# Row scans of the later sets in two halves, and weight blocks converted at one pace

## The chip, the cores and the metric

The kernel runs on one core of a Trainium2 chip. The metric is the device time of one execution in microseconds (us). The core has five engines that run unsynchronised, each with its own queue of instructions in program order: TensorE (PE; its weight loads are listed as PEld), VectorE (DVE), ScalarE (ACT), GpSimd (POOL) and SyncE (SP), which here only issues transfers (DMA).

## What is computed

Two stages, all in float32. The first is a recurrence over 768 steps for 4 x 8 heads of width 40; the second a two-layer MLP ("MoE" in the names) on 3072 rows of 320:

```python
for t in range(S):
    y[:, :, t] = np.einsum('bhd,bhde->bhe', rt, state)
    Sa = np.einsum('bhde,bhe->bhd', state, at)
    state = state * wt[:, :, None, :] - np.einsum('bhd,bhe->bhde', Sa, bt) + np.einsum('bhd,bhe->bhde', vt, kt)
x = y.transpose(0, 2, 1, 3).reshape(B * S, H * D)
h = x @ w_in                                     # 320 -> 2048
g = np.where(h >= 1, h, np.where(h <= -1, 0.0, (h + 1) ** 2 / 4))
out = g @ w_out                                  # 2048 -> 320
```

## The kernel before

The recurrence is done in 24 chunks of 32 steps. Six sets of four chunks are prepared one after the other, each in three stages. *Rows* (`prelude`, L241): for each of four parts of eight steps, the running products P of w and their reciprocals come from two scans on VectorE, forward and reversed, over a tile of 40 groups of 10 columns (`scan`, L227, its instruction is L235); zeros at both ends of a group restart the product, so the 40 groups do not depend on each other. GpSimd multiplies a, k and b by the results (L273, L281, L289) and stores the part to DRAM (`scr`, L290). *ab*: rows are loaded back from `scr` (L304), transposed (L325), multiplied pairwise on TensorE (L336) and copied to `pairs` (L343). *inv*: a triangular inversion of `pairs`, for sets 1 and on as 62 products and differences on GpSimd (L363, L369); `adopt` (L376) puts its result in place for the next four chunks.

The chain of the recurrence (`chain`, L504, one generator for each chunk and half of the heads) and the MoE (`moe`, L628) run beside this. The MoE takes 64 steps at a time; a step k of it makes `ph` on TensorE (L637), the gate on ACT, DVE, ACT and POOL (L647, L648, L650, L653 for `gh`, L654 for `gl`), and then 12 second products (L668) with the two weight blocks `w2_2k` and `w2_2k+1`, of step k - 1, whose last four need `gl`.

Weights arrive as 64-bit floats and are converted in 28 blocks (`weights`, L742; 12 of `w_in`, then 16 of `w_out`, named `w2_0` to `w2_15`). A block is two ACT instructions (L751, L755), one on DVE (L759), a cast on ACT (L771) and the low part on POOL (L772; some early ones on DVE); it ends two blocks later in the program than it begins, and its end issues the raw load of the block five ahead (L739, on SP).

Everything is emitted in one order by hand. The main loop calls `fill` (L917) four times a chunk; a fill advances the clock `now` by 2.5 and has six turns. In each turn it emits MoE matmuls, advances the weight generator when the sum of `PACE` says so (each block is three such steps), and calls `background` (L411). That takes the stage that is furthest behind its due share in its window (`WINDOWS`) and runs its generator to the next `yield`, whose value counts as work done; `size` is a stage's total. If the MoE's first group needs a block that is not yet converted, it advances the weight generator itself (`needs`).

Of the kernel before, what the change touches and what calls it, by code (L numbers as in the profile page):

```python
# [20 lines left out]
NB, NHD, D, L = 4, 8, 40, 32  # L21
# [7 lines left out]
    rows=[(0, 0), (24, 43), (46, 64), (70, 90), (106, 130)],  # L29
    ab=[(0, 0), (44, 55), (68, 84), (95, 119), (135, 159)],  # L30
    inv=[(2, 28), (55.5, 79), (85, 118), (121, 158), (161, 198)],
)

AHEAD = 5
PACE = (0.8, 1.0)

SHARE = (1.4, 0.6) * 2
SLOTS = len(SHARE)
# [1 line left out]
ROWS_W = (2, 2, 4, 2, 6, 6, 8)  # L40
AB_W = (6, 26, 6, 3, 8, 30)
INV_W = 12
INV_STEP = [0.45 + (j + 1) * (31 - j) / 256 for j in range(31)]
# [12 lines left out]
def rwkv_moe_kernel(ctx: ExitStack, tc: tile.TileContext, r, k, v, w, a, b, w_in, w_out, ident_d, mask_d, out):  # L56
# [28 lines left out]
    wz = const.tile([128, D, 10], F32, name="wz")  # L85
    dz = const.tile([128, D, 10], F32, name="dz")
# [49 lines left out]
    def copy_rv(s, part, c, n=1):  # L136

        x, o = ((r, O_R), (v, O_V))[part]
        nc.sync.dma_start(
            scr[s][0 : NH * 128].rearrange("(h x) e -> h x e", x=128)[:, L * c : L * (c + n), o : o + D],  # L140
            x.rearrange("b h t e -> (b h) t e")[:, 128 * s + L * c : 128 * s + L * (c + n), :],
        )
# [84 lines left out]
    def scan(out, d0, d1, step=1):  # L227


        def line(x):  # L230
            x = x.rearrange("p e t -> p (e t)")
            (pp, pn), (st, n) = x.ap
            return x if step == 1 else bass.AP(x.tensor, x.offset + (n - 1) * st, [[pp, pn], [-st, n]])

        nc.vector.tensor_tensor_scan(  # L235
            out=line(out), data0=line(d0), data1=line(d1), initial=0.0, op0=ALU.mult, op1=ALU.add
        )
# [3 lines left out]
    def prelude(s):  # L241

        R = arena.rearrange("p (t x) -> p t x", x=160)
        kt, P, at, bt = (R[:, :, 40 * i : 40 * i + 40] for i in range(4))
        rows_ = lambda x: x.rearrange("p e t -> p t e")

        def load(n, s, part):
            if n == "w":
                t = work.tile([128, 10 * D], F32, tag="ld_w", name="ld_w")
            else:  # L250
                t = work.tile([128, 8 * D], F32, tag="ld_x", name=f"ld_{n}", bufs=2)
            x = t[:, 0 : 8 * D].rearrange("p (t e) -> p t e", e=D)
            nc.sync.dma_start(x, srcs[n][:, 4 * s : 4 * s + 4, 8 * part : 8 * part + 8, :])
            return (t, x) if n == "w" else x

        wl, al, kl = ahead.pop(s) if s in ahead else [load(n, s, 0) for n in "wak"]
        yield 10
        for part in range(4):
            ts_ = slice(8 * part, 8 * part + 8)
            then = (s, part + 1) if part < 3 else (s + 1, 0)  # L260
            more = then[0] < NS
            nc.scalar.copy(rows_(wz)[:, 1:9], wl[1])
            yield ROWS_W[0]
            Pc = wl[0].rearrange("p (e t) -> p e t", t=10)
            if part == 0:
                nc.vector.memset(dz[:, :, 0], -1.0)
            scan(Pc, wz, dz)
            yield ROWS_W[1]
            if part < 3:
                nc.vector.tensor_copy(dz[:, :, 0], Pc[:, :, 8])  # L270
            nc.vector.reciprocal(dz[:, :, 9], Pc[:, :, 8])
            nc.scalar.copy(P, rows_(Pc)[:, 1:9])
            nc.gpsimd.tensor_mul(at, al, rows_(Pc)[:, 0:8])  # L273
            yield 1
            scan(wz, wz, dz, -1)
            rec = rows_(wz)[:, 2:10]
            copy_rv(s, 0, part)
            yield ROWS_W[2]
            bl = load("b", s, part)
            yield ROWS_W[3]  # L280
            nc.gpsimd.tensor_mul(kt, kl, rec)  # L281
            if more:
                wl = load("w", *then)
            yield ROWS_W[4]
            if more:
                al = load("a", *then)
            copy_rv(s, 1, part)
            yield ROWS_W[5]
            nc.gpsimd.tensor_mul(bt, bl, rec)  # L289
            nc.gpsimd.dma_start(scr[s][0 : NH * 128, 80:240].rearrange("(p t) x -> p t x", t=L)[:, ts_, :], R)  # L290
            nc.gpsimd.memset(wz[:, :, 0::9], 0.0)
            yield ROWS_W[6]
            if more:
                kl = load("k", *then)
        if more:
            ahead[s + 1] = wl, al, kl
# [82 lines left out]
    def staged(key, needs, work_of):  # L379
        for s in range(2 if key != "inv" else 0, NS):  # L380
            if needs:
                drain(needs, s)
            total = 0
            for d in work_of(s):
                total += d
                yield d
            if s:
                size[key] = total
            done[key] = s
            yield 0  # L390

    turned_in, turned_out = set(), set()
    done, size, spent = dict(rows=1, ab=1), dict(rows=10 + 4 * (1 + sum(ROWS_W)), ab=2 * AB_W[5] + 4 * AB_W[0] + 8 * (2 + sum(AB_W[1:4])), inv=INV_W + 2 * sum(INV_STEP)), {}
    back = {k: staged(*a) for k, a in dict(
        rows=("rows", None, prelude), ab=("ab", "rows", ab_set), inv=("inv", "ab", invert)).items()}

    def drain(key, s):
# [13 lines left out]
    def background(n):  # L411

        due = []
        for key in ("inv", "ab", "rows"):
            for s in range(1, NS):
                a, b = window(key, s)
                if a < n <= b:
                    drain(key, s - 1)
                    at = spent.setdefault((key, s), [0])
                    due.append((key, s, at, size[key] * (gone(n) - gone(a)) / (gone(b) - gone(a))))  # L420
        while True:
            due = [(k, s, at, to) for k, s, at, to in due if done[k] < s and at[0] < to]
            if not due:
                return
            key, _, at, _ = max(due, key=lambda x: x[3] - x[2][0])
            at[0] += next(back[key])
# [368 lines left out]
    def pull(gen, n=1):  # L795
        for _ in range(n):
            if next(gen, "end") == "end":
                return False
        return True
# [94 lines left out]
    now = [0]  # L894
    due = [0]
# [5 lines left out]
    def feed(cols):  # L901

        if not Xs:
            return
        owed[0] += cols * (not idle[0])
        while owed[0] > 0:
            d = next(mgen)
            owed[0] = 0 if d is None else owed[0] - d
            idle[0] = d is None

    def catch_up():

        for f in deferred:
            f()
        deferred.clear()

    def fill():  # L917

        catch_up()
        for k in range(6):  # L920
            feed(1280)
            if first:
                first.pop(0)()
            due[0] += PACE[now[0] >= 20]
            while due[0] > 0:
                pull(wgen)
                due[0] -= 1
            background(now[0] + 10 / SLOTS * (k + 1) / 6)
        now[0] += 10 / SLOTS

    for c in range(NC + 1):
# [9 lines left out]
        if c < NC:  # L941
            if c and c % 4 == 0:
                adopt(c // 4)
            for j in (0, 1) if c else (2, 0, 1):
                turn(c, 1, j)
        fill()
        stage(c - 1, 1)
        stage(c, 0)
# [7 lines left out]
        if nxt:  # L956
            load_cg(c + 1, 0)
            turn(c + 1, 0, 2)
        fill()
        for g, (t0, nt) in enumerate(groups):  # L960
            if t0 + nt == 32 * c:
# [8 lines left out]
        if nxt:  # L970
            for j in (0, 1):
                turn(c + 1, 0, j)
        fill()
        stage(c, 0)
        stage(c, 1)
# [43 lines left out]
```

## Time and profile before

| | us |
|---|---|
| median of 3 runs | 791.98 (785.94 to 795.64) |
| the profiled execution, its own time | 791.32 |
| its span, first to last instruction | 789.5 |
| PE busy | 680.1 (86%) |
| DVE busy | 590.6 (75%) |
| ACT busy | 472.6 (60%) |
| POOL busy | 449.7 (57%) |

How the rows below are read. A row of the table by stretches gives the stretch, its length, and for PE, PEld, DVE, ACT and POOL the busy time with the number of instructions, then the granted TensorE clock as a share of full speed, the DMA engines' busy share and GB/s. A row of the groups by line gives line, engine, operation, output<-inputs, shapes and count, then busy time and the mean of one in ns, then the idle time before it and what ended that. A row of the timeline gives start and length in us, engine, line, operation, and in brackets the idle time before it with what ended it. The chain of waits follows from the last instruction back to what released each step.

### The profile page before, as it was taken

What the parts mean: (1) busy time and instruction counts of PE and PEld (TensorE: products, weight loads), DVE (VectorE), ACT (ScalarE), POOL (GpSimd) and SP (SyncE); (2) the same over time, 40 slices, a digit from 0 to 9 for tenths busy, and PEclk for the clock granted to TensorE, in tenths of its full rate; (3) what the DMA queues carried; (4) which work ended last, traced back from release to release, by engine and by line L of the source; (5) the groups of instructions that cost most, each with busy time, mean ns of one, the idle gap of its engine ahead of it and who ended that gap; (6) DMA issues with size and microseconds to landing.
All of it is one profiled execution on the core that took longest, in us unless ns stands there. A gap on an engine that the chain in (4) does not pass through costs nothing.

```text
span 789.5 us, 35564 instructions
## 1 busy us (share of the span) xinstructions
PE 680.1 (86%) x15360; PEld 626.2 (79%) x15360; DVE 590.6 (75%) x1329; ACT 472.6 (60%) x1016; POOL 449.7 (57%) x615
## 2 busy tenths in 40 slices
PE   4635756688899888899989899999999999999997
PEld 4624645677778777789978889899999999999996
DVE  6998988699678686878778887688877787776211
ACT  5636755576465565557557575574765656655544
POOL 1242899866236998557758686554566642222332
PEclk9775566799689999799999999999999999999999
DMA  8898976876776666576348573442433324330100
GB/s 299 224 233 171 208 163 163 224 178 167 158 169 154 150 145 142 135 180 144 87 91 193 151 186 70 110 92 53 103 74 88 73 64 93 73 86 20 34 23 18
DMA packets 180524, 102.35 MB, mean 130 GB/s; under 512 B 124760, under 2 KB 172056, under 8 KB 180368
## 3 DMA queue, kind: packets, MB, share of 16 engines
q1 hardware_dynamic: 175216, 83.53, 47.2%
q0 software_dynamic: 4992, 16.39, 7.3%
q8 instruction: 121, 1.98, 1.1%
q14 instruction: 35, 0.29, 0.1%
q10 hardware_dynamic: 160, 0.16, 0.1%
HBM read 70.88 MB, written 27.53 MB: 125 GB/s over the span
## 4 chain that ended last, share of the span: by engine, by line
PE 61%; DVE 12%; POOL 10%; issue 6%; ACT 6%; DMA 4%; SPq 0%; POOLq 0%; ACTq 0%; DVEq 0%
PE ph L637 20%; PE po L668 18%; PE p L556 5%; PE p L545 3%; PE p L585 3%; PE p L485 3%; PE p L519 3%; PE p L529 3%; POOL lw L369 2%; POOL lw L363 2%; DMA scr<-arena 2%; POOL w L772 2%; PE p L336 1%; DMA tiab<-scr 1%; POOL gl L654 1%
## 5 line engine op out<-in xcount | busy, mean ns | idle before, releaser
L637 PE MATMUL ph<-X,w 120*128 120x256 f32 x1536 | 224.7, 301 | 5.1 <-DMA X<-Y 3.7
L654 POOL TENSOR_TENSOR gl<-gt,gh 128x512 fp32r<-128x512 f32 x95 | 122.1, 1285 | 163.8 <-ACT gh L653 156.9
L637 PEld LDWEIGHTS ph<-X,w 120*128 120x128 f32 x1536 | 203.1, 202 | 12.7 <-issue 3.0
L668 PE MATMUL po<-w,gh 128*128 128x320 f32 x768 | 135.7, 319 | 8.4 <-ACT gh L653 7.8
L650 DVE SCALAR_TENSOR_TENSOR gt<-gt,ph 128x512 f32<-128x512 f32 x95 | 65.0, 685 | 94.0 <-ACT gt L648 85.8
L668 PEld LDWEIGHTS po<-w,gh 128*128 128x128 f32 x768 | 118.4, 195 | 10.7 <-ACT gh L653 9.2
L653 ACT CAST gh<-gt 128x512 fp32r<-128x512 f32 x95 | 58.8, 619 | 85.1 <-DVE gt L650 75.5
L647 ACT ACTIVATE gt<-ph,half_c 128x512 f32<-128x512 f32 x95 | 65.2, 687 | 54.6 <-PE ph L637 53.8
L369 POOL TENSOR_TENSOR lw<-lw 128x31 f32<-128x31 f32 (+15 forms) x155 | 88.9, 573 | 8.4
L363 POOL TENSOR_TENSOR lw<-lw 128x31 f32<-128x31 f32 (+15 forms) x155 | 87.1, 562 | 8.0
L563 DVE SCALAR_TENSOR_TENSOR cg<-p,pr 40x160 f32<-40x160 f32 x184 | 59.1, 321 | 34.0 <-PE p L556 31.7
L668 PE MATMUL po<-w,gl 128*128 128x320 f32 x384 | 75.2, 318 | 10.5 <-POOL gl L654 10.5
L497 DVE TENSOR_TENSOR cg<-p,mask 32x256 f32<-32x256 f32 x192 | 80.5, 419 | 4.4 <-PE p L485 0.9
L540 ACT ACTIVATE cg<-p 32x160 f32<-32x160 f32 x192 | 56.5, 295 | 38.0 <-DVE cg L536 24.3
L668 PEld LDWEIGHTS po<-w,gl 128*128 128x128 f32 x384 | 61.1, 192 | 13.6 <-POOL gl L654 13.4
L556 PE MATMUL p<-cg 128*64 128x72 f32 (+1 forms) x1536 | 64.5, 242 | 0.0
L576 POOL TENSOR_TENSOR Y<-yt,Y 128x256 fp32r<-128x256 f32 x48 | 36.0, 750 | 49.1 <-ACT Y L575 49.0
L536 DVE SCALAR_TENSOR_TENSOR cg<-p,mask 32x128 f32<-32x128 f32 x192 | 55.2, 288 | 9.5 <-ACT cg L540 3.9
L648 ACT ACTIVATE gt<-gt 128x512 f32<-128x512 f32 x95 | 60.0, 632 | 3.0
L556 PEld LDWEIGHTS p<-cg 128*64 128x64 f32 x1536 | 58.9, 151 | 0.4 <-issue 0.4
L545 PEld LDWEIGHTS p<-cg 128*40 128x40 f32 x1472 | 36.0, 130 | 21.5 <-ACT cg L540 13.4
L545 PE MATMUL p<-cg 128*40 128x40 f32 x1472 | 42.2, 218 | 12.5 <-ACT cg L540 12.5
(105 smaller groups left out, 1103.1 us busy)
## 6 DMA issues: line engine op xcount, KB each, us to landing
ti<-scr SPq DMA_DIRECT2D x96, 200.0 KB
scr<-arena POOLq DMA_DIRECT2D x16, 640.0 KB, 5.4
cg<-scr SPq DMA_DIRECT2D x96, 80.0 KB
X<-Y SPq DMA_DIRECT2D x36, 160.0 KB
scr<-wide SPq DMA_DIRECT2D x8, 640.0 KB
w<-in_moe_w_out_dram SPq DMA_DIRECT2D x16, 320.0 KB
tiab<-scr SPq DMA_DIRECT2D x28, 160.0 KB
cg<-scr SPq DMA_DIRECT2D x96, 40.0 KB
```

What stands on the lines that cost most here:

```text
L363: eng.tensor_mul(t3, W3[:, 0:n, j : j + 1].broadcast_to([128, n, m]), L3[:, j + 1 :, j].unsqueeze(1).broadcast_to([128, n, m]),)
L369: eng.tensor_sub(W3[:, 0:n, j + 1 :], W3[:, 0:n, j + 1 :], t3)
L497: nc.vector.tensor_tensor(out=cg[q, f::2, C_X : C_X + 64][:, 4 * i : 4 * i + 4].rearrange("p h (j x) -> p h j x", x=32), in0=ps[quarter(f, ...
L545: nc.tensor.matmul(pst[er[h % 2], h // 2, :], lhsT=cg[:, h, C_S : C_S + D], rhs=cg[:, h, C_G : C_G + D], start=True, stop=True)
L556: nc.tensor.matmul(psv[h // 8][64 * f : 64 * f + 64, h // 2 % 4, 0:n3], lhsT=cgw[:, h * CW + C_G : h * CW + C_G + 64], rhs=cg[:, h, C_R : ...
L563: nc.vector.scalar_tensor_tensor(out=cn[er[f], f::2, C_S : C_S + D][:, halves[i]], in0=psv[i][er[f], :, 32:72], scalar=-1.0, in1=pr[er[f], ...
L637: nc.tensor.matmul(phs[k % 2][:, n * j : n * j + n], lhsT=wt[0, f // 4, wi // 2][:, wi % 2, fs], rhs=Xs[g][:, xi, :], start=i == 0, stop=i ...
L647: nc.scalar.activation(gt, ph, AF.Relu, bias=half_c, scale=0.5)
L648: nc.scalar.activation(gt, gt, AF.Square)
L650: nc.vector.scalar_tensor_tensor(out=gt, in0=gt, scalar=1.0, in1=ph, op0=ALU.min, op1=ALU.max)
L654: nc.gpsimd.tensor_sub(gl, gt, gh.bitcast(F32))
L668: nc.tensor.matmul(pos[i], lhsT=x[:, ts_], rhs=w, start=q == 0 and k == 0, stop=end)
```

## The change

Both scans of a part, L235, are issued as two scans over 20 of the 40 groups each, with a `yield 1` after each half, at which the planner chooses again; the size of a row set is set to match. The pace of the weight steps, which was 0.8 a turn until `now` is 20 and 1.0 from then on, is 0.8 throughout.

```diff
-PACE = (0.8, 1.0)
+PACE = 0.8
...
+        halves = slice(0, D // 2), slice(D // 2, D)
...
-            scan(Pc, wz, dz)
+            for es in halves:
+                scan(Pc[:, es], wz[:, es], dz[:, es])
+                yield 1
             yield ROWS_W[1]
...
-            scan(wz, wz, dz, -1)
+            for es in halves:
+                scan(wz[:, es], wz[:, es], dz[:, es], -1)
+                yield 1
...
-    done, size, spent = dict(rows=1, ab=1), dict(rows=10 + 4 * (1 + sum(ROWS_W)), ab=2 * AB_W[5] + 4 * AB_W[0] + 8 * (2 + sum(AB_W[1:4])), inv=INV_W + 2 * sum(INV_STEP)), {}
+    done, size, spent = dict(rows=1, ab=1), dict(rows=10 + 4 * (5 + sum(ROWS_W)), ab=2 * AB_W[5] + 4 * AB_W[0] + 8 * (2 + sum(AB_W[1:4])), inv=INV_W + 2 * sum(INV_STEP)), {}
...
-            due[0] += PACE[now[0] >= 20]
+            due[0] += PACE
```

Line numbers in the changed program are higher by 1 to 5. On TensorE the order of instructions is the same in both.

The first place is POOL's queue around the first `gl` of the MoE (about 144 to 152 us in the profile). `w2_...` are weight blocks, `lw` the inversion, `arena` the rows of a part. Before:

```order
L369 TENSOR_TENSOR lw_84<-lw_84 128x31
L772 TENSOR_TENSOR w2_5_2091<-tiab_81,w2_5_2091 128x320
L289 TENSOR_TENSOR arena_78<-ld_b_1963,wz_79 128x8x40
L290 DMA scr2_107<-arena_78 128x8x160
L291 MEMSET wz_79 128x40x2
L772 TENSOR_TENSOR w2_6_2110<-tiab_81,w2_6_2110 128x320
L654 TENSOR_TENSOR gl_2117<-gt_2107,gh_2116 128x512
L772 TENSOR_TENSOR w2_7_2205<-tiab_81,w2_7_2205 128x320
L273 TENSOR_TENSOR arena_78<-ld_a_1979,ld_w_1973 128x8x40
```

And now:

```order
L374 TENSOR_TENSOR lw_84<-lw_84 128x31
L777 TENSOR_TENSOR w2_4_2090<-tiab_81,w2_4_2090 128x320
L294 TENSOR_TENSOR arena_78<-ld_b_1964,wz_79 128x8x40
L295 DMA scr2_107<-arena_78 128x8x160
L296 MEMSET wz_79 128x40x2
L659 TENSOR_TENSOR gl_2104<-gt_2099,gh_2103 128x512
L777 TENSOR_TENSOR w2_5_2183<-tiab_81,w2_5_2183 128x320
L276 TENSOR_TENSOR arena_78<-ld_a_1973,ld_w_1967 128x8x40
```

Two blocks fewer stand ahead of the first `gl`, and the one between the memset and `gl` is gone from there. The second place is DVE's queue in the fill that starts near 184 us, with the last reverse scan of set 2 (`wz<-wz,dz`); L376 is `adopt`, L464 and L467 are transposes of the chain. Before:

```order
L650 SCALAR_TENSOR_TENSOR gt<-gt,ph_63 128x512
L271 RECIPROCAL dz<-ld_w 128x40
...
L376 STREAM_TRANSPOSE tinv<-lw 128x32x32
L464 STREAM_TRANSPOSE cg_85<-ti_83 64x8x32 x2
L467 STREAM_TRANSPOSE ev<-ti_83 128x512
L235 SCALAR_TENSOR_TENSOR wz<-wz,dz 128x400
L650 SCALAR_TENSOR_TENSOR gt<-gt,ph_64 128x512
```

And now:

```order
L381 STREAM_TRANSPOSE tinv<-lw 128x32x32
L469 STREAM_TRANSPOSE cg_85<-ti_83 64x8x32 x2
L472 STREAM_TRANSPOSE ev<-ti_83 128x512
L764 SCALAR_TENSOR_TENSOR tiab<-tiab,pairs 128x320
L274 RECIPROCAL dz<-ld_w 128x40
L235 SCALAR_TENSOR_TENSOR wz<-wz,dz 128x200 x2
L764 SCALAR_TENSOR_TENSOR tiab<-tiab,pairs 128x320
L655 SCALAR_TENSOR_TENSOR gt<-gt,ph_64 128x512
```

The reciprocal that the scan reads and one step of a weight block (L759 of before, L764 now) now stand between the transposes and the scan; a second one stands between the scan's halves and the gate. The third place is POOL's queue around the sixth `gl` (near 192 us), where the last blocks now end:

```order
L659 TENSOR_TENSOR gl_2801<-gt_2787,gh_2800 128x512
L581 TENSOR_TENSOR Y_945<-yt_2699,Y_945 128x2x4x32
L777 TENSOR_TENSOR w2_13_2901<-tiab_81,w2_13_2901 128x320
L777 TENSOR_TENSOR w2_14_2916<-tiab_81,w2_14_2916 128x320
L777 TENSOR_TENSOR w2_15_2924<-tiab_81,w2_15_2924 128x320
L659 TENSOR_TENSOR gl_2946<-gt_2935,gh_2945 128x512
```

Before, the same three stood ahead of the fifth `gl`:

```order
L576 TENSOR_TENSOR Y_945<-yt_2432,Y_945 128x2x4x32
L772 TENSOR_TENSOR w2_13_2650<-tiab_81,w2_13_2650 128x320
L772 TENSOR_TENSOR w2_14_2663<-tiab_81,w2_14_2663 128x320
L772 TENSOR_TENSOR w2_15_2676<-tiab_81,w2_15_2676 128x320
L654 TENSOR_TENSOR gl_2684<-gt_2669,gh_2683 128x512
```

So they moved by one MoE step and a fill.

## Rows read from the trace of the kernel before

**Rows 1.** The page, part 1: the span, and busy time of each engine.

```profile
span 789.5 us, 35564 instructions
PE 680.1 (86%) x15360; PEld 626.2 (79%) x15360; DVE 590.6 (75%) x1329; ACT 472.6 (60%) x1016; POOL 449.7 (57%) x615
```

**Rows 2.** Busy time by stretches, two stages.

```profile
120.00:160.00 40.00, 28.75 (x548) 25.77 (x550) 30.68 (x64) 24.57 (x59) 33.19 (x46) 0.70 0.72 191
...
460.00:789.00 329.00, 320.35 (x6666) 301.12 (x6665) 215.66 (x514) 196.63 (x425) 157.06 (x211) 0.99 0.32 72
```

**Rows 3.** Busy time by stretches: five fills with conversions, six dense fills.

```profile
137.03:185.36 48.33, 36.65 (x686) 32.58 (x685) 40.28 (x76) 34.03 (x77) 36.54 (x45) 0.89 0.76 192
...
351.66:389.72 38.06, 38.06 (x938) 35.40 (x937) 30.87 (x76) 26.13 (x59) 28.44 (x45) 1.00 0.57 122
```

**Rows 4.** Chain by line, 120 to 147.85 and 159 to 183; L772 (DVE, POOL) there.

```profile
by line: POOL w L772 23.3%; POOL lw L369 15.9%; POOL lw L363 12.2%; issue 9.7%; PE p L556 7.3%; PE p L545 5.5%; POOL arena L281 4.6%; DMA scr<-arena 4.2%; POOL arena L289 3.6%; POOL arena L273 3.6%; POOL Y L576 3.0%; ACT ss L550 2.7%; ACT p
...
by line: issue 20.6%; DVE ld_w L235 7.8%; DVE tiab L759 7.6%; ACT tiab L751 7.2%; DVE cg L563 7.1%; ACT pairs L755 6.6%; ACT w L771 6.3%; DVE gt L650 5.9%; ACT ti L310 4.9%; ACT gt L647 3.3%; DVE cg L464 3.3%; DVE cg L587 3.1%; DVE ev L467 
...
159.00:183.00 24.00, 0.00 (x0) 6.97 (x7) 1.00 0.79 194
```

**Rows 5.** Timeline at the first `gl`: a scan, the product, PE.

```profile
147.12 2.81 DVE L235 TENSOR_TENSOR_SCAN ld_w<-wz,dz 128x400 f32<-128x400 f32 x1 [1.08 <-POOL wz L291]
...
147.80 1.27 POOL L654 TENSOR_TENSOR gl<-gt,gh 128x512 fp32r<-128x512 f32 x1
...
149.12 1.17 PE L668 MATMUL po<-w,gl 128*128 128x320 f32 x3 [4.62 <-POOL gl L654]
```

**Rows 6.** Timeline from set 2's last reverse scan to its first pair matmuls.

```profile
187.83 0.95 DVE L235 TENSOR_TENSOR_SCAN wz<-wz,dz 128x400 f32<-128x400 f32 x1
...
189.45 0.62 ACT L653 CAST gh<-gt 128x512 fp32r<-128x512 f32 x1 [3.18 <-DVE gt L650]
...
191.27 0.92 POOL L290 DMA_DIRECT2D scr<-arena  x1 [0.30 <-POOL arena L289]
...
192.14 1.34 PE L668 MATMUL po<-w,gh 128*128 128x320 f32 x8
...
193.56 0.75 POOL L576 TENSOR_TENSOR Y<-yt,Y 128x256 fp32r<-128x256 f32 x1
...
198.88 0.76 PE L668 MATMUL po<-w,gh 128*128 128x320 f32 x4
203.18 0.67 PE L336 MATMUL p<-ea 40*32 40x32 f32 x32 [3.55 <-DVE ea L325]
```

**Rows 7.** Instructions of L759: ns of one, least, median and most; first and last.

```profile
L759 DVE SCALAR_TENSOR_TENSOR tiab<-tiab,pairs x16: 449/646/2630, 113.2 to 178.2; 128x320 uint32<-128x320 uint32 x16
```

**Rows 8.** Groups by line: the forward scans, and prices of single instructions.

```profile
L369 POOL TENSOR_TENSOR lw<-lw 128x31 f32<-128x31 f32 (+15 forms) x155 | 88.9, 573 | 8.4
...
L235 DVE TENSOR_TENSOR_SCAN ld_w<-wz,dz 128x400 f32<-128x400 f32 x16 | 18.7, 1166 | 2.6 <-POOL wz L291 1.3 <-ACT wz L262 0.7 <-issue 0.4
...
L271 DVE RECIPROCAL dz<-ld_w 128x40 f32<-128x40 f32 x16 | 6.3, 396 | 0.1
...
L173 DVE TENSOR_TENSOR wide<-wide,X 128x160 f32<-128x160 f32 x7 | 2.3, 325 | 0.2
...
L178 DVE TENSOR_TENSOR wide<-wide,wide 128x1240 f32<-128x1240 f32 x1 | 1.4, 1449 | 0.0
```

**Rows 9.** The page, part 4: the chain of waits by engine.

```profile
PE 61%; DVE 12%; POOL 10%; issue 6%; ACT 6%; DMA 4%; SPq 0%; POOLq 0%; ACTq 0%; DVEq 0%
```

**Rows 10.** Timeline: scans inside which a POOL instruction starts, first and last; one example.

```profile
130.18 0.99 DVE L235 TENSOR_TENSOR_SCAN ld_w<-wz,dz 128x400 f32<-128x400 f32 x1 [0.45 <-ACT wz L262]
...
288.64 1.35 DVE L235 TENSOR_TENSOR_SCAN ld_w<-wz,dz 128x400 f32<-128x400 f32 x1 [0.26 <-ACT wz L262]
289.22 1.24 POOL L369 TENSOR_TENSOR lw<-lw 128x247 f32<-128x247 f32 x1
...
453.15 0.98 DVE L235 TENSOR_TENSOR_SCAN ld_w<-wz,dz 128x400 f32<-128x400 f32 x1
```

## The prediction

> **What bounds the kernel now.** I read the page's busy shares first [rows 1]: TensorE (PE) is busy 86% of a span of 789.5 us. The table by stages shows where the rest is [rows 2]: from 460 us to the end PE works 320.35 of 329 us at a granted clock of 0.99 of full speed; from 120 to 160 us it works 28.75 of 40 us at 0.70. Both edits act between 120 and 460 us (conversions to 182 us, scans from 130 to 458 us), so time can only be won or lost there; the changed program issues the same PE instructions in the same order.
>
> How much is there? Steps of the schedule (fills) that carry little besides the chain and the MoE matmuls take 38.06/6 = 6.34 us, PE full [rows 3]. The five fills from 137.03 to 185.36 us, which carry conversions, row sets and the first MoE steps, take 48.33/5 = 9.67 us. Their excess is 5 x 3.3 = 16.6 us.
>
> What fills the excess is in the chain and the waits. Before 147.85 us the chain runs through GpSimd (POOL): L772, the low part of a converted block, is 23.3% of 27.85 us, 6.5 us for the seven blocks `w2_0` to `w2_6`, with the inversion (L363, L369) beside it [rows 4]. Then PE stands 4.62 us for the first `gl` of the gate [rows 5]. From 159 to 183 us the chain goes through VectorE (DVE) and ScalarE (ACT): L759, L751, L755 and L771, all conversion, hold 7.6 + 7.2 + 6.6 + 6.3 = 27.7% of 24 us, 6.6 us, while seven blocks end (L772 x7) [rows 4]. At 199 to 203 us PE stands 3.55 us for the pair matmuls of set 2, at the end of scan, POOL products, store to `scr`, load into `lw` [rows 6].
>
> **Conversions at 0.8 throughout.** From the eighth fill on a fill converts 1.6 blocks and not 2, until the MoE asks for a block itself. Nothing is removed, 28 blocks stay; they move later. The order shows where to. Ahead of the first `gl` POOL has two L772 fewer (the one just before it is `w2_4`, before it was `w2_6`); between the second and the sixth `gl` it has six and not seven; three stand after the sixth, past 192 us.
>
> First place: 6.5 us of chain over seven blocks is 0.93 us each. Two fewer bring the first `gl` 1.9 us earlier, and the 4.62 us wait has room for it: **-1.9 us**. Second place: 6.6 us over seven blocks is 0.95 us of chain a block, one block fewer: **-0.95 us**. Third place, the cover: POOL ends L576 at 193.56 + 0.75 us, and the product that needs `w2_13` starts on PE at 198.88 us [rows 6]. Three L772 of 0.93 us, 2.8 us, fit in those 4.6 us, and the later two blocks are not needed before the next fill. I cost them at nothing; without the cover, 2.8 us.
>
> Fourth place, a loss: in the fill at 184 us L759 and the reciprocal L271 now stand between the transposes and the last reverse scan of set 2. That scan ran at 187.83 us, its result went through POOL to the store at 191.27 us, and PE waited at the end of that line until 203.18 us [rows 6]. So the line gets later by one L759 (646 ns, median), one L271 (396 ns) and the scan's extra fixed part (0.158 us, next paragraph) [rows 7, 8]: **+1.2 us**. The gate behind them is late by one L759 more, 1.85 us; its `gh` was cast by 190.07 us and PE took it at 192.14 us [rows 6], so that costs nothing, with little to spare.
>
> **Scans in halves.** 32 scans of 400 columns (the 16 forward ones take 1166 ns in the mean) become 64 of 200 [rows 8]. No row shows a 200-column scan. Below, halving is perfect and costs nothing; above, each new instruction pays the fixed part of a DVE instruction. Two rows give that part: 160 columns take 325 ns, 1240 take 1449 ns, so 1.041 ns a column and 158 ns fixed [rows 8]. I take 158 ns, since it comes from the same engine and the same kind of operand: 32 x 0.158 = 5.1 us of DVE time (0 to 5.1). How much of it lies on the path? The chain gives DVE 12% of the span and POOL 10% [rows 9], 94.7 and 79.0 us, nearly all before 460 us: 21% and 17% of that stretch. 5.1 x 0.21 = **+1.1 us**.
> [...]
>
> The second effect is who gets between the halves. The scan at 147.12 us took 2.81 us and ended 0.86 us after POOL's L654 had: it stood behind POOL. The reverse holds at 288.64 us: a POOL product that started inside a scan took 1.24 us, where such products average 573 ns [rows 5, 8, 10]. In 18 of the 32 scans (the first at 130.18, the last at 453.15 us) a POOL instruction starts while the scan runs. With two halves it can run at the seam: the second half then waits some 0.57 us, while POOL starts about half a scan, 0.58 us, earlier. DVE loses 18 x 0.57 = 10.3 us, 2.2 us of it on the path; POOL gets 10.4 us, 1.8 us on the path: **+0.4 us**, between -1.8 (DVE's loss hidden) and +2.2 (POOL's gain useless).
> [...]
>
> The four new yields a part (5 where there was 1 in the size) move row steps within a fill or to the next one: on SyncE's queue some loads of `w`, `a` and `v` fall behind the next `ti` and `cg` loads, by one group of six issues. No row shows a reader of such a load waiting. I cost it at nothing; the cover is the distance to the reader (L262 on ACT for `w`), about a fill, and without it ACT, which runs in order, would stand there with the gate's L647 behind it, up to a dense fill's 6.3 us each time.
>
> **Sum.** -1.9 - 0.95 + 1.2 + 1.1 + 0.4 = -0.15 us on the profiled execution's 791.32 us (span 789.5 and 1.8 around it): **791.2 us**. It lies 0.8 us below the median of the runs shown, 791.98, which themselves spread over 9.7 us.
>
> **Rivals.**
> *Faster.* Conversions are the cause of the whole excess in the five fills: a fifth less of them takes a fifth of 16.6 us, 3.3 us, and the first wait of 4.62 us goes entirely: 791.3 - 7.9 = 783.4 us. For it speaks the share of L772 in the chain; against it that the three blocks come back where the `lw` line is late already.
> *Slower, the other side.* The seams are given to POOL and nothing comes back: DVE's 5.1 + 10.3 = 15.4 us. In fills with scans DVE's next instruction is often the gate L650 or L587 of the chain, on which PE waits; if half of it reaches PE, 791.3 + 7.7 = 799 us, if all, 806.7 us. It decides from half the seams on the path. Against it: [rows 9] gives DVE a fifth of that stretch.
> *Late blocks.* `w2_13` comes more than 4.6 us late and PE stands for it; three blocks' L772, 2.8 us, bare on the path, and the fourth place's 1.2 us once more: about 795 us.
> *No effect of the halves.* The order shows that in most places the two halves stand side by side on DVE, with nothing put between them, so nothing gets past earlier on DVE itself; that is inside my forecast.
>
> **How the numbers follow.** Forecast (within some 4 us of 791.2) 0.44, faster 0.25, slower 0.20, late blocks 0.08, more than these 0.03. The range runs from the faster rival's 783 to just past the slower one's 799: 783 to 802; outside stay the full price of the seams and a gain larger than the excess explains. A measurement of this kernel can tell about 2% (15.8 us) from no change. A gain of that size needs nearly all of the 16.6 us of excess: 0.03. A loss of that size needs all 15.4 us of the seams and more: 0.04. Within 2%: 0.93.
>
> **What would show it.** In the changed profile the 200-column scans should average 0.5 to 0.9 us, 0.158 us over half of the old ones where POOL is quiet; DVE busy up by about 5 us and more if seams are given away; POOL's products L363/L369 shorter in the mean; PE's wait for the first `gl` near 2.7 us; the last L772 near 196 us and PE not waiting for it; PE's wait for set 2's pair matmuls about a microsecond longer. I am wrong if PE waits on `gh` or on the chain's DVE steps grow in most fills with scans, or if the granted clock between 120 and 200 us moves by more than a tenth, since my sum holds it as it is.

## The result, and the profile after

The changed kernel takes 784.04 us in the median of 20 runs (776.92 to 791.07); the kernel before, in 20 runs beside it, 791.04 us (785.45 to 798.14). The ratio is 0.9904, 95% interval [0.9884, 0.9924]: 7.6 us less, between 6.0 and 9.2 (the two medians differ by 7.0). By the 2% at which this kernel was to be called changed, that is no change, which had the chance of 0.93. But it is not the forecast's mechanism: the sum was -0.15 us, and 784.04 lies outside the forecast's own 4 us around 791.2. The range of 783 to 802 holds it by one microsecond, because its lower end is the rival *Faster*, 783.4. That this rival's number came is luck: it is made of a first wait that goes entirely and of fewer conversions, while the wait stayed at 3.02 us (below) and pace alone gave 4.1 us.

The profiled execution after took 787.5 us with a span of 785.7, 3.5 above its median. First the page: span, busy time of each engine, and the costliest groups that answer to [rows 1, 8] (busy us, mean ns of one, idle time before).

```profile
span 785.7 us, 35598 instructions
PE 675.9 (86%) x15360; PEld 622.0 (79%) x15360; DVE 591.8 (75%) x1361; ACT 472.0 (60%) x1016; POOL 443.7 (56%) x615
...
L374 POOL TENSOR_TENSOR lw<-lw 128x31 f32<-128x31 f32 (+15 forms) x155 | 87.1, 562 | 8.2
L368 POOL TENSOR_TENSOR lw<-lw 128x31 f32<-128x31 f32 (+15 forms) x155 | 85.5, 552 | 8.0
```

DVE issues 32 instructions more and is busy 1.2 us longer; POOL is busy 6.0 us less. PE is busy 4.2 us less with the same 15360 matmuls, while the rest of the span (109.8 us, it was 109.4) is as long as before: between these two executions the difference is in how long the matmuls took, not in how long PE stood. That bears on the clock, see below. The same groups by line, for the scans:

```profile
L235 DVE TENSOR_TENSOR_SCAN ld_w<-wz,dz 128x200 f32<-128x200 f32 x32 | 21.3, 697 | 4.9 <-ACT wz L263 2.8 <-POOL wz L296 1.4 <-issue 0.4
L235 DVE TENSOR_TENSOR_SCAN wz<-wz,dz 128x200 f32<-128x200 f32 x32 | 21.1, 696 | 0.4
```

The forward scans took 18.7 us [rows 8] and take 21.3. Next the timeline at the first `gl` (answers to [rows 5]) and along set 2's line (answers to [rows 6]).

```profile
146.20 1.28 POOL L659 TENSOR_TENSOR gl<-gt,gh 128x512 fp32r<-128x512 f32 x1
147.54 1.43 PE L673 MATMUL po<-w,gl 128*128 128x320 f32 x4 [3.02 <-POOL gl L659]
...
185.76 0.45 DVE L764 SCALAR_TENSOR_TENSOR tiab<-tiab,pairs 128x320 uint32<-128x320 uint32 x1
186.13 0.40 DVE L274 RECIPROCAL dz<-ld_w 128x40 f32<-128x40 f32 x1
186.56 1.04 DVE L235 TENSOR_TENSOR_SCAN wz<-wz,dz 128x200 f32<-128x200 f32 x2
190.20 0.92 POOL L295 DMA_DIRECT2D scr<-arena  x1 [0.30 <-POOL arena L294]
192.57 0.85 PE L673 MATMUL po<-w,gl 128*128 128x320 f32 x4 [1.78 <-POOL gl L659]
197.92 0.85 PE L673 MATMUL po<-w,gh 128*128 128x320 f32 x4
201.36 0.68 PE L341 MATMUL p<-ea 40*32 40x32 f32 x32 [2.59 <-DVE ea L330]
```

The instructions of L777, a converted block's low part (ns of one: least, median, most; first and last start):

```profile
L777 POOL TENSOR_TENSOR w<-tiab,w x16: 856/872/1153, 125.6 to 195.3; 128x320 fp32r<-128x320 f32 x16
```

The first wait for `gl` is 3.02 us, it was 4.62. The last low part starts at 195.3 us, and the product at 197.92 does not wait for a block. The pair matmuls of set 2 start 1.8 us earlier than before, after a wait of 2.59 us where it was 3.55. The stages (PE, PEld, DVE, ACT, POOL busy, then granted clock), as in [rows 2]:

```profile
120.00:160.00 40.00, 29.96 (x578) 27.04 (x580) 31.63 (x71) 22.55 (x54) 31.33 (x46) 0.67 0.71 186
460.00:785.00 325.00, 318.51 (x6664) 299.27 (x6662) 216.40 (x516) 197.06 (x425) 157.79 (x212) 1.00 0.33 73
```

PE issues 578 matmuls between 120 and 160 us where it issued 548, at a slightly lower granted clock (0.67, it was 0.70). In the end stage PE is busy 98% of the time, as it was (97%).

### The profile page after: what moved, and what is told of

It reads as the page before. It is cut to its first block, busy times and chain, and to the rows that moved or that the text cites. A ratio compares the mean times of both kernels' runs of the same rounds, so it can differ in the third digit from the quotient of the medians.

```text
span 785.7 us, 35598 instructions
## 1 busy us (share of the span) xinstructions
PE 675.9 (86%) x15360; PEld 622.0 (79%) x15360; DVE 591.8 (75%) x1361; ACT 472.0 (60%) x1016; POOL 443.7 (56%) x615
## 4 chain that ended last, share of the span: by engine, by line
PE 51%; DVE 5%; POOL 3%; DMA 2%; issue 1%; ACT 1%; SPq 0%; ACTq 0%; DVEq 0%; POOLq 0%
PE ph L642 18%; PE po L673 16%; PE p L561 4%; PE p L550 3%; PE p L590 2%; PE p L524 2%; PE p L490 2%; PE p L534 2%; DMA tiab<-scr 1%; PE p L341 1%; POOL gl L659 1%; DVE wz L235 1%; DVE ld_w L235 1%; DVE tinv L381 1%; DVE cg L568 0%
## 5 line engine op out<-in xcount | busy, mean ns | idle before, releaser
L642 PE MATMUL ph<-X,w 120*128 120x256 f32 x1536 | 220.0, 297 | 5.1 <-DMA X<-Y 3.9
L642 PEld LDWEIGHTS ph<-X,w 120*128 120x128 f32 x1536 | 198.3, 198 | 12.9 <-issue 4.8
L374 POOL TENSOR_TENSOR lw<-lw 128x31 f32<-128x31 f32 (+15 forms) x155 | 87.1, 562 | 8.2
L368 POOL TENSOR_TENSOR lw<-lw 128x31 f32<-128x31 f32 (+15 forms) x155 | 85.5, 552 | 8.0
L673 PE MATMUL po<-w,gl 128*128 128x320 f32 x384 | 75.8, 320 | 10.4 <-POOL gl L659 10.4
L545 ACT ACTIVATE cg<-p 32x160 f32<-32x160 f32 x192 | 56.6, 295 | 35.5 <-DVE cg L541 21.3
L541 DVE SCALAR_TENSOR_TENSOR cg<-p,mask 32x128 f32<-32x128 f32 x192 | 55.2, 287 | 10.4 <-ACT cg L545 5.2
```

The source lines that it names most:

```text
L368: eng.tensor_mul(t3, W3[:, 0:n, j : j + 1].broadcast_to([128, n, m]), L3[:, j + 1 :, j].unsqueeze(1).broadcast_to([128, n, m]),)
L374: eng.tensor_sub(W3[:, 0:n, j + 1 :], W3[:, 0:n, j + 1 :], t3)
L642: nc.tensor.matmul(phs[k % 2][:, n * j : n * j + n], lhsT=wt[0, f // 4, wi // 2][:, wi % 2, fs], rhs=Xs[g][:, xi, :], start=i == 0, stop=i ...
L673: nc.tensor.matmul(pos[i], lhsT=x[:, ts_], rhs=w, start=q == 0 and k == 0, stop=end)
```

## The experiments

All kernels were timed against the kernel before in five rounds; a ratio in us is taken of 791. "Choice points" below are the points, made by `yield 1`, at which the planner may turn to something else. The expectations name three theories: A, the later conversions bring the gain; B, the seams between half scans do; C, the row steps do that the choice points move. The prediction had the choice points at nothing, a little gain from pace and a little loss from the split.

**Pace alone.**

```diff
-PACE = (0.8, 1.0)
+PACE = 0.8
...
-            due[0] += PACE[now[0] >= 20]
+            due[0] += PACE
```

> The kernel before with the one pace of 0.8, scans whole. If the later conversions bring the gain (theory A), it runs 6 to 8 us below the kernel before, about 784 us. If the gain comes from the seams between half scans (theory B) or from the row steps that the new yields move (theory C), it lies within 2 us of before, about 790 us. My sum gave the pace -1.65 us.

Measured: 0.9948 [0.9911, 0.9985], -4.1 us [-7.0, -1.2]. Less time, by an interval that leaves out zero, and more than the 1.65 us of the prediction, though these lie inside the interval. It is also between the 6 to 8 us of theory A and the 2 us of the others: pace is a part of the gain.

**Scans alone, with their choice points.** The changed kernel at the old pace.

```diff
-            scan(Pc, wz, dz)
+            for es in halves:
+                scan(Pc[:, es], wz[:, es], dz[:, es])
+                yield 1
...
```

> Half scans with their yields and the larger size, but the pace of before (0.8, then 1.0). Theory A: no gain, 790 to 793 us (my sum gave the halves +1.5 us). Theories B and C: 784 to 787 us.

Measured: 0.9964 [0.9932, 0.9997], -2.9 us [-5.4, -0.2]. The prediction had a small loss here, +1.5 us.

**The split alone.** Both halves side by side, no choice point between or behind, old size and pace.

```diff
-            scan(Pc, wz, dz)
+            for es in halves:
+                scan(Pc[:, es], wz[:, es], dz[:, es])
...
```

> Half scans side by side, no yield between or behind them, size and pace of before: on every engine the order of before, with 32 more scans on VectorE. Theory B: it keeps most of the gain of the halves, 784 to 787 us. Theory C: no gain, and the fixed part of 32 more instructions costs 0 to 2 us: 791 to 793 us. Theory A: the same, 791 to 793 us.

Measured: 1.0025 [0.9990, 1.0059], +2.0 us [-0.8, +4.7]. So the gain of the run before is not from halving, and theory B falls.

**The choice points alone.** Whole scans, two choice points behind each, size as in the change, old pace.

```diff
             scan(Pc, wz, dz)
+            yield 1
+            yield 1
...
```

> Whole scans, each followed by two yields of 1, with the larger size; pace of before. Only the places of the row steps in the order move. Theory C: it keeps the gain of the halves with yields, 784 to 787 us. Theories A and B: within 2 us of before, 789 to 793 us.

Measured: 0.9969 [0.9931, 1.0006], -2.5 us [-5.5, +0.5]. By itself this decides nothing, since zero is inside; with the next run it does.

**The change without the split.** The choice points alone, and pace 0.8.

> Whole scans with two yields behind each and the larger size, and the one pace of 0.8: the change without the split of the instruction. If the three parts add up as measured one by one (pace -4.1 us, moved row steps -2.5 us, split +2.0 us), it runs 784 to 787 us, at or slightly below the changed kernel (784.0). If the split is what makes the moved row steps pay, 788 us, like the pace alone.

Measured: 0.9915 [0.9878, 0.9951], -6.7 us [-9.7, -3.9]. The two parts add up (-4.1 - 2.5 = -6.6), and within the interval the kernel is as fast as the changed one, without a single half scan.

**Pace only ahead of the first gate.** Pace 0.8 until `now` is 27.5 and not 20, 1.0 from then on: the first `gl` has its two blocks fewer, and what follows keeps its pace.

```diff
-            due[0] += PACE[now[0] >= 20]
+            due[0] += PACE[now[0] >= 27.5]
```

> The kernel before with the pace of 0.8 held until the clock of the schedule is 27.5 and 1.0 from there: two blocks fewer ahead of the first gl, as in the change, but no conversion moved past the sixth gl; scans whole. If the pace's gain is the early gl (POOL's queue ahead of it), it keeps 2 to 4 us of the 4.1: 788 to 790 us. If the gain comes from fewer conversions in each of the later fills, it keeps under 1 us: 791 to 792 us.

Measured: 1.0009 [0.9974, 1.0044], +0.7 us [-2.1, +3.5]. The first `gl` did come early (row below: 145.12 us, 2.7 earlier than in [rows 5]) and brought nothing that shows at the end, though the interval leaves room for some 2 us.

```profile
145.12 1.28 POOL L654 TENSOR_TENSOR gl<-gt,gh 128x512 fp32r<-128x512 f32 x1
...
146.45 1.44 PE L668 MATMUL po<-w,gl 128*128 128x320 f32 x4 [3.29 <-POOL gl L654]
```

**Slower still, and half way.** `PACE = (0.8, 0.7)` and `PACE = (0.8, 0.9)`.

> The kernel before with the pace 0.7 from 20 on: one more block leaves the queue ahead of the first gl, and in the fills behind it blocks come one later again until the MoE asks for them itself; the last three stay where 0.8 put them. If the gain grows with what leaves the crowded fills, 785 to 788 us. If PE then waits for late blocks (the rival of late blocks), above 790 us.

> The kernel before with the pace 0.8 and then 0.9, between the two. 0.8 measured -4.1 us (interval -7.1 to -1.2), 0.7 measured +0.9 us (-2.2 to +4.0). If the gain grows with the thinning until PE waits for late blocks, about half, 789 to 790 us. If it is a matter of which engine's turn each block meets, there is no order in it, and the value can lie anywhere from 786 to 794 us.

Measured: 1.0011 [0.9972, 1.0051], +0.9 us [-2.2, +4.0] at 0.7, and 0.9972 [0.9937, 1.0007], -2.2 us [-5.0, +0.6] at 0.9. Over 0.7, 0.8, 0.9, 1.0 the time is +0.9, -4.1, -2.2, 0, so the gain does not go on growing the later the blocks come; but 0.7 and 0.8 lie 5.0 us apart with an uncertainty of some 4, and how much worse 0.7 is these runs do not say.

**Four quarters.** Scans of 10 groups side by side, no choice points.

```diff
+        halves = [slice(10 * i, 10 * i + 10) for i in range(4)]
...
```

> Each scan as four of 10 groups side by side, no yields; size, pace and order of before. The price of a seam by dose: the halves cost 2.0 us (interval -0.8 to 4.7) with one seam a scan, so three seams should cost 6 us, 796 to 800 us, if the extra instructions lie on the path as I reckoned (1.5 us a seam: 795 to 797 us). If the seams hand POOL as much as they take from VectorE, it stays within 2 us of before.

Measured: 1.0058 [1.0017, 1.0098], +4.6 us [+1.3, +7.8]. With no, one and three seams a scan the time is 0, +2.0 and +4.6 us, so one more seam in all 32 scans costs about 1.5 us together, as the expectation had it.

**Choice points behind the forward scan only, behind the reverse scan only, and doubled.** Pace 0.8; two `yield 1` and a size smaller by 8 in the first two, two pairs of `yield 2` in the third.

> Whole scans, pace 0.8, the two yields only behind the forward scan (size 3 a part). On SyncE's queue two places differ from the pace alone: one r copy falls behind a group of ti and cg loads, and in the fifth set the tiab loads come ahead of a and v. With both pairs of yields three more loads or groups (w, a, v) fall behind ti and cg. Pace alone measured -4.1 us, with both pairs of yields -6.7 us. If the extra gain is the order on SyncE, this stays near the pace alone, 787 to 789 us; if it is VectorE's order behind the forward scan, 784 to 786 us.

> The same with the two yields only behind the reverse scan; SyncE's order as in the run with the forward ones. If the extra gain is the order on SyncE, 787 to 789 us; if it is what comes behind the reverse scan (kt on POOL, the b load, later by two counts), 784 to 786 us.

> Whole scans, pace 0.8, both pairs of yields at 2 and not 1 (size 9 a part): the row steps move further in the same sense, on SyncE too (30 lines of difference to the pace alone, where the single yields have 18). If moving the row steps later is good in itself, at or below the run with single yields, 780 to 785 us; if its gain was only where these steps happened to fall, anywhere from 783 to 792 us.

Measured: 0.9906 [0.9873, 0.9938], 0.9908 [0.9873, 0.9944] and 0.9945 [0.9912, 0.9979], that is -7.4, -7.3 and -4.3 us. Either pair gives all of what both give; for the doubled ones no gain over pace alone shows, though the -6.7 of the single ones lies inside their interval. One theory falls with this: that SyncE's loads of `w`, `a` and `v` coming later is what pays. They move so only with both pairs. On SyncE both single pairs share two other moves (one copy of `r` falls behind a group of `ti` and `cg` loads; in the fifth set the `tiab` loads come ahead of `a` and `v`); no run separates these from the order on VectorE.

## Why the prediction was right, and where it was wrong

The call of no change within 2% held, since 7.6 us is half of the 15.8 us that it allowed. The sum behind it did not: its gain from pace was too small, it had no gain from the choice points, and its loss from the split did not show; that they add up to -0.15 us is chance. The runs make a table of two paces by four forms of the scan (ratio to the kernel before):

| pace | whole | whole, choice points behind | halves side by side | halves, choice points |
|---|---|---|---|---|
| 0.8, then 1.0 | 1 | 0.9969 | 1.0025 | 0.9964 |
| 0.8 throughout | 0.9948 | 0.9915 | not run | 0.9904 |

Differences between neighbours, in us: pace -4.1, -4.3 and -4.7; choice points -2.5, -2.6 and -4.8; split +2.0, -0.4 and -0.9. One such difference is uncertain by 3 to 4 us, so no single one proves much; that three agree does for pace and choice points, and says that the split has no gain of its own that could be seen. The prediction had -1.65 for pace (its four places together), 0 for the choice points and +1.5 for the split.

**The choice points, costed at nothing.** This is the step that failed. I asked only whether a reader of a late load would wait, a loss, and not what the moved steps leave behind. One fill shows what. It lies near 280 to 297 us and holds the example of [rows 10]. The timeline of the kernel before, from a set's transposes `ea` to the matmul of the chain that waits for the copy of their products (`pairs`), with the two scans of a later set's part between; the first of these two scans is in [rows 10]:

```profile
286.33 0.73 DVE L325 STREAM_TRANSPOSE ea<-tiab 128x256 f32<-128x256 f32 x2
287.51 0.77 DVE L325 STREAM_TRANSPOSE ea<-tiab 128x256 f32<-128x256 f32 x2 [0.46 <-PE p L336]
290.85 1.45 DVE L235 TENSOR_TENSOR_SCAN wz<-wz,dz 128x400 f32<-128x400 f32 x1
291.41 1.30 POOL L363 TENSOR_TENSOR lw<-lw 128x240 f32<-128x240 f32 x1
292.97 0.62 ACT L653 CAST gh<-gt 128x512 fp32r<-128x512 f32 x1 [0.93 <-DVE gt L650]
293.49 0.26 ACT L343 COPY pairs<-p 128x128 f32<-128x128 f32 x1
293.81 0.46 PE L485 MATMUL p<-cg,ev 40*32 40x32 f32 x32 [2.65 <-ACT pairs L343]
```

The same in the kernel with choice points behind the reverse scan only, and whole scans:

```profile
283.79 0.73 DVE L327 STREAM_TRANSPOSE ea<-tiab 128x256 f32<-128x256 f32 x2
284.69 0.99 DVE L235 TENSOR_TENSOR_SCAN ld_w<-wz,dz 128x400 f32<-128x400 f32 x1
284.73 1.43 POOL L371 TENSOR_TENSOR lw<-lw 128x252 f32<-128x252 f32 x1
285.60 0.75 DVE L327 STREAM_TRANSPOSE ea<-tiab 128x256 f32<-128x256 f32 x2
286.78 1.01 DVE L235 TENSOR_TENSOR_SCAN wz<-wz,dz 128x400 f32<-128x400 f32 x1
288.60 0.62 ACT L655 CAST gh<-gt 128x512 fp32r<-128x512 f32 x1 [0.81 <-DVE gt L652]
289.12 0.26 ACT L345 COPY pairs<-p 128x128 f32<-128x128 f32 x1
289.43 0.46 PE L487 MATMUL p<-cg,ev 40*32 40x32 f32 x32 [0.82 <-ACT pairs L345]
```

Before, DVE did the four transposes, idling 0.46 us on PE between the pairs, and then both scans, each with a POOL product inside (1.35 and 1.45 us). Now the first scan stands between the two pairs of transposes, where DVE idled. From the first transpose to PE's matmul it takes 5.64 us where it took 7.48, and PE waits 0.82 us and not 2.65. The way to PE is through ACT: the copy of `pairs` stands in its queue behind the gate's cast, which waits for the gate step on DVE, and that step stands behind both scans. Of the 1.84 us, 0.72 is idle time of DVE that is gone (0.46 above and 0.26 in [rows 10]) and 0.80 the scans, which took 0.99 and 1.01 us: here the POOL products that start inside them are the long ones, 1.43 us (L371) and 1.72 us (L273), where the kernel before shows 0.69 and 1.04 us for two of the same line of code and shape (287.72 and 290.41 us). The changed kernel has the same order here, but with halves:

```profile
284.46 0.73 DVE L330 STREAM_TRANSPOSE ea<-tiab 128x256 f32<-128x256 f32 x2
285.37 1.74 DVE L235 TENSOR_TENSOR_SCAN ld_w<-wz,dz 128x200 f32<-128x200 f32 x2
285.84 0.83 POOL L374 TENSOR_TENSOR lw<-lw 128x252 f32<-128x252 f32 x1
287.03 0.74 DVE L330 STREAM_TRANSPOSE ea<-tiab 128x256 f32<-128x256 f32 x2
288.71 1.87 DVE L235 TENSOR_TENSOR_SCAN wz<-wz,dz 128x200 f32<-128x200 f32 x2
292.09 0.46 PE L490 MATMUL p<-cg,ev 40*32 40x32 f32 x32 [2.58 <-ACT pairs L348]
```

7.63 us: the 1.84 that the choice point gives are taken back by the split, whose two pairs of halves hold DVE 1.74 and 1.87 us where whole scans held it 0.99 and 1.01. In this fill, then, the kernel without the split is the better one, and it does show what each part does; the whole runs can't tell the two kernels apart. The order of this fill recurs, by the same two rows of every trace: 5.6 to 6.3 us in the five kernels with whole scans and choice points, 7.3 to 7.5 in the five with whole scans and none, 7.6 and 7.7 with halves and choice points, 8.1 with halves side by side and 8.9 with quarters.

It is not the whole account. In kernels with halves the choice points shorten this fill by 0.3 to 0.4 us only, and yet they gave 4.8 us there; what the changed kernel gains by them must lie elsewhere. The kernel with doubled choice points has this order as well (5.93 us) and shows no gain over pace alone. Which other placements pay stays open: they were not tried one by one.

**Pace, the term mis-sized.** The mechanism can be seen where I put it. The chain transposes `pr` once a half chunk (48 rows); between the 5th and the 12th lies the stretch with conversions. Before and with pace alone:

```profile
96.16 0.71 DVE L469 STREAM_TRANSPOSE pr<-ti 128x512 f32<-128x512 f32 x1
...
214.10 0.71 DVE L469 STREAM_TRANSPOSE pr<-ti 128x512 f32<-128x512 f32 x1
```

```profile
97.11 0.71 DVE L469 STREAM_TRANSPOSE pr<-ti 128x512 f32<-128x512 f32 x1
...
211.59 0.71 DVE L469 STREAM_TRANSPOSE pr<-ti 128x512 f32<-128x512 f32 x1
```

117.9 and 114.5 us. By the same two rows of each trace, the four at the old pace (all but the quarters) take 117.5 to 120.7 us (mean 119.0), the six at 0.8 throughout 113.2 to 116.3 (mean 115.1): 3.9 us less, against -1.65 in the sum and -4.1 to -4.7 in the runs. The granted clock is a little higher in the six (0.78 in the mean, 0.74 in the four), but it does not order the stretches: the shortest of these stretches, 113.2 us, has 0.74 (choice points behind the reverse scan), while pace 0.9 has 0.81 and takes 117.8. By the sum's own places:
- The first, -1.9: `gl` came 1.6 us earlier and the wait shrank by 1.6. Right in its place: the run with pace 0.8 only up to there has 116.0 us in this stretch, 1.9 less than before. It is about half of what the whole change of pace gives there, so the rest of that change matters too.
- The fourth, +1.2, has the wrong sign in the end. Both instructions do stand ahead of set 2's last reverse scan (185.76 and 186.13 us), but the scan itself ran at 186.56 us, it was 187.83 [rows 6]. The transposes at the fill's start (`adopt`) show why, before and then now:

```profile
184.41 2.04 DVE L376 STREAM_TRANSPOSE tinv<-lw 128x1024 f32<-128x1024 f32 x1
...
182.28 2.09 DVE L381 STREAM_TRANSPOSE tinv<-lw 128x1024 f32<-128x1024 f32 x1
```

  From them to the scan it does take 0.86 us longer (4.28, it was 3.42), but they begin 2.13 us earlier: I added two instructions to a fill that I held where it was. That the fewer conversions of the fills before it brought it forward is the likely reason, not shown by itself. The rival *Faster* had that thought (a fifth of the excess, 3.3 us), and I gave it a quarter.
- The third, the cover: right, nothing waits for a late block. A new wait of 1.78 us for the sixth `gl` (192.57 us) stands beside it, which I had not named.

Why 0.7 shows no gain was not traced to an instruction. What I can say is that its trace has 116.7 us in this stretch, nearly as good as at 0.8.

**The halves.** The direction was right and both sizes were too large. The fixed part, taken as 158 ns: by the instructions of L235 before and after,

```profile
L235 DVE TENSOR_TENSOR_SCAN ld_w<-wz,dz x16: 949/992/2808, 130.2 to 453.1; 128x400 f32<-128x400 f32 x16
L235 DVE TENSOR_TENSOR_SCAN wz<-wz,dz x16: 949/1054/1503, 132.7 to 457.7; 128x400 f32<-128x400 f32 x16
```

```profile
L235 DVE TENSOR_TENSOR_SCAN ld_w<-wz,dz x32: 520/574/1586, 130.6 to 454.2; 128x200 f32<-128x200 f32 x32
L235 DVE TENSOR_TENSOR_SCAN wz<-wz,dz x32: 531/575/1305, 133.9 to 458.9; 128x200 f32<-128x200 f32 x32
```

two halves cost 91 and 113 ns over one whole by the least (2 x 520 - 949, 2 x 531 - 949), 156 and 96 by the median. The prediction's 158 is just above the highest of the four.

The scans' busy time was 37.0 us (18.7 forward [rows 8], 18.3 reverse by the same view) and is 42.4: +5.4, in the other two kernels with halves +6.5 and +7.4, where the sum had 15.4. Less the fixed part of 32 more scans, the seams took DVE an estimated 1.4 to 4 us (by the two means of the figures above, 102 and 126 ns a scan) and not 10.3. What POOL got is there too: its inversion products (L363, L369 before) take 172.6 to 173.3 us in the three kernels with halves and 175.6 to 177.8 in those with whole scans; 3 to 4 us, not 10.4. The prediction's 0.57 us for such a product is a mean over sixteen widths; the 247-column one of its example took 0.67 us with no scan beside it, in the kernel with choice points behind the reverse scan. The rows of the last two fences of the fill show one exchange: with a whole scan the POOL product beside it took 1.43 us, with halves 0.83, and DVE 0.75 us longer. The rival *Slower* priced each seam as given away; by the 1.4 to 4 us most were not, and 4.6 us at three seams a scan is far from its 7.7 at one.

**The clock.** The prediction held it, and the bound it set itself was kept: between 120 and 200 us the granted clock is 0.81 where it was 0.83, and lower, not higher. Over the whole span it did move. Its mean is 0.913 in the 20 runs of the changed kernel and 0.908 in the 101 runs of the kernel before that stood beside the experiments. 0.005 of 788 us is an estimated 4 us of TensorE at full speed, as much as PE's 4.2 us of busy time above. So a good part of the 7.6 us may have come by way of the clock, for which the sum had no term. Whether the new order itself brings the higher clock no run separates.

**The signs.** Of those that the prediction named, the mean of a half scan (0.70 us), the shorter POOL products (562 and 552 ns, they were 573 and 562), the first wait (3.02 us for 2.7) and the last low part (195.3 us for 196) came. DVE's busy time did not rise by 5 us but by 1.2, and PE's wait for set 2's pair matmuls got shorter and not longer. PE's waits on `gh` between 120 and 460 us did not grow (6.0 us, they were 7.8).

No kernel run is faster than the changed one by more than the interval; the change with whole scans and one pair of choice points (0.9906, 0.9908) equals it with fewer instructions.

## What to carry to other kernels

In a kernel whose order comes from a planner, price an edit's new choice points as an edit of their own: look in the order for steps that moved into a gap where an engine idles (here 0.46 us of DVE between two pairs of transposes), for a gain as well as for a loss. A step that is delayed can bring forward what stood behind it (the transposes of `adopt` began 2.13 us earlier), so work out where the next fill starts before adding to it. Compare the granted clock of two profiles stretch by stretch before reading a few us as waits. A scan split in two took 91 to 156 ns more here by the least and the median, and a seam more in all 32 scans cost about 1.5 us of the whole; try the reordering without the split first.

## What was not expected of the hardware

The same code can take several us more or less. From about 232 to 362 us (13th to 21st `pr` transpose) the kernels that differ in pace alone have the same instructions in the same order on every engine as the kernel before, all conversions being over. Yet this stretch takes 130.6 us before, 130.5 at pace 0.7, 128.5 with pace 0.8 only ahead of the first gate and 125.9 with pace alone. Busy time between the 13th and the 21st transpose, the kernel before and then pace alone:

```profile
232.01:362.61 130.60, 116.31 (x2543) 105.73 (x2543) 101.38 (x220) 74.61 (x162) 94.19 (x135) 0.92 0.67 156
231.35:357.22 125.87, 111.54 (x2527) 101.32 (x2526) 100.99 (x221) 74.24 (x162) 94.44 (x135) 0.93 0.68 158
```

DVE, ACT and POOL are busy alike in both; PE is busy 4.8 us less, which is about the whole difference. The largest piece of it is a fill near the middle. The kernel before, then pace alone: the last of two waits of PE, a product of the MoE behind it, and the stretch with the granted clock.

```profile
327.41 0.33 PE L336 MATMUL p<-ea 40*32 40x32 f32 x16 [0.88 <-DVE ea L325]
332.75 2.71 PE L637 MATMUL ph<-X,w 120*128 120x256 f32 x11
327.60:334.90 7.30, 7.30 (x162) 6.60 (x151) 6.79 (x16) 4.60 (x12) 3.28 (x4) 0.56 0.38 95
...
324.43 0.33 PE L336 MATMUL p<-ea 40*32 40x32 f32 x16 [0.88 <-DVE ea L325]
328.10 1.56 PE L637 MATMUL ph<-X,w 120*128 120x256 f32 x11
324.20:331.50 7.30, 6.86 (x203) 6.09 (x204) 7.09 (x17) 5.41 (x14) 3.67 (x4) 1.00 0.43 107
```

PE stood twice just before, 1.28 and 0.88 us in both kernels alike. In the kernel before the granted clock then fell to half of full speed, the lower of the two levels in the trace's records (0.50 from 331.00 to 334.90 us, 0.56 in the mean of these 7.3 us), and the eleven matmuls took 2.71 us; with pace alone it stayed at the upper one (1.00) and they took 1.56. From the product behind the wait to the next pair matmuls that is 7.72 us against 4.90. Over the whole stretch, by the trace's records of the clock, the lower level was on for 21.4 us before, 21.3 at pace 0.7, 20.5 with pace 0.8 ahead of the first gate and 17.1 with pace alone: the same order as the four times. So equal work with equal waits met the clock's fall in one execution and not in another, and a few us of a single profile can be that; the runs of one kernel spread over 10 us and more (785.45 to 798.14 before). Why it fell in one and not in the other these traces do not show, and whether part of pace's gain at the end comes this way stays open. A difference of a few us between two single profiles can't be read as the effect of an edit; one that recurs in four or six kernels, as above, can be, if the clock is looked at beside it.
